# Stage two's operand moved to 98 partitions, written in 34- and 30-row transfers and read in one

## The chip, the cores and the metric

The kernel runs on one core of one Trainium2 chip. The metric is the device time of one execution in microseconds (us). A kernel is one program for five engines, each with an instruction order of its own: TensorE (PE, matmuls and weight loads), VectorE (DVE), ScalarE (ACT), GpSimd (POOL) and SyncE (SP). SP, ACT and GpSimd also issue the transfers, which 16 DMA engines carry out.

## The reference

The input x has 8 batches of 3072 x 256 numbers. Each batch goes through a Fourier transform along both axes, of which the real part is kept; every one of the 24,576 rows then goes through a layer of three parallel products.

```python
X = np.fft.fft(x, axis=1)
X = np.fft.fft(X, axis=2)
attn = X.real.astype(np.float32)            # (8, 3072, 256)
x = attn.reshape(24576, 256)
h = np.maximum(np.maximum(x @ w1, x @ w2), x @ w3)   # 256 -> 768
out = (h @ w_out).astype(np.float32)                 # 768 -> 256
```

## The kernel before

The transform along the 3072 rows is done in two stages, 96 x 32; the one along the 256 columns is folded into the weights (`product`, `prep_second`), as cosine and sine tables `md` and `nmd` times w1, w2 and w3. Only half of the spectrum is computed; the other half is a mirror image, for which the layer has a plus and a minus form (`unit_plus`, `unit_minus`).

A batch b passes these steps, which the class `Mix` holds:

- `load_x` (L106): GpSimd loads x into `xt`, in bf16, in two halves of two transfers (rows forward into partitions 0 to 31, reversed into 32 to 63). `mirror` (L113), on VectorE, fills partitions 64 to 127.
- `s` (L317), stage one: seven groups of matmuls with the small table `tabz`; ScalarE copies the sums to `tb`, 128 partitions: 64 rows q for even s, 64 for odd s, where s runs from 0 to 48.
- `y` (L329): SP writes `tb` to a DRAM buffer `db` of 49 x (64 x 128), in two transfers of 64 rows for each stretch of s, in packets of 256 B. The last 30 of the 64 rows are the sine part, the first 34 the cosine part (the sine part's first and last pair are zero and not stored).
- `z` (L338): SP reads `db` back into `yb`, now with s in the partitions: 49 rows of the cosine part from partition 0, 49 of the sine part from partition 64, each in a transfer of 48 rows and one of a single row. The partitions between are zero from the start.
- `x0` (L352): two small matmuls of the column 0 of x, into `x0s`; `c` (L361) copies `x0s` into column 0 of `yb`, on GpSimd (ScalarE for the first part of batch 0).
- `k` (L364) and `end`: stage two, matmuls of `yb` with the tables `te_tab` and `to_tab`, into `tE` and `tO`. The tables come from `angles` on VectorE and `tables` on ScalarE, in three parts of 512 columns.

The layer works on three blocks of 512 columns of tE and tO in each batch, six units each, so 18 units a batch. In a unit TensorE does the plus and minus matmuls (L388, L389, L396), ScalarE and VectorE take the maximum (L402, L403), and matmuls with `wout_bf` (L412) of the block before follow, ten at a time (`l2_some`). When a slot of 128 columns is done, VectorE adds it up into `ot` (L440, six buffers), GpSimd issues an indirect store of one half (L445) and sets a mark (L449), and SP issues the direct stores of the other (L452).

The order of all this is written out by hand, and each engine keeps it: `plan` gives to each unit what else is issued there. For batches 1 to 6 the steps for the next batch stand as follows (unit in front):

```python
ahead = {1: ("s0", "s1"), 2: ("s2", "y0", "s3"), 3: ("s4", "s5"), 4: ("s6", "y1", "x"),
         7: ("z",), 11: ("c",), **late}
```

`late` puts stage two into units 13 to 17; the x loads of the batch after next stand in units 9 to 12 and its mirrors in 14 to 17. In batch 0, preparing batch 1, they are later and closer: y0 in unit 7, y1 and x0 in 9, z in 11, c in 12.

The head of the program does the same for batch 0 in four stretches of s, with `warm_up` matmuls in TensorE's holes, makes the weight products of the first halves of w1, w2, w3 (`load_w(0)`), and loads the second halves (`load_w(1, landed[1])`) only when a read of `db` has landed. The products of the second halves (`prep_first`) and the tables of columns 512 on come in units 0 to 2 of batch 0.

Transfers of SP use eight completion semaphores in turn, so that a transfer waits for the one eight before it.

Of the kernel before, what the change touches and what calls it, by code (L numbers as in the profile page):

```python
# [10 lines left out]
BF16 = mybir.dt.bfloat16  # L11
INT32 = mybir.dt.int32
AX = mybir.ActivationFunctionType
ALU = mybir.AluOpType
# [29 lines left out]
def kernel(  # L44
# [9 lines left out]
    nc = tc.nc  # L54
# [6 lines left out]
    NHALF = 1536  # L61
    UNITS = 3 * NJC
    NS = 49
    RI = 17

    E_ = mybir.EngineType
    ctx.enter_context(tc.manual_schedule(
# [1 line left out]

    consts = ctx.enter_context(tc.tile_pool(name="consts", bufs=1))  # L70
    ps_f = ctx.enter_context(tc.tile_pool(name="ps_f", bufs=2, space=bass.MemoryType.PSUM))
    d_pool = ctx.enter_context(tc.tile_pool(name="dbuf", bufs=2, space=bass.MemoryType.DRAM))
    t_pool = ctx.enter_context(tc.tile_pool(name="tbuf", bufs=2))

    xt = [consts.tile([128, NS * 256], BF16, name=f"xt{i}", tag=f"xt{i}") for i in range(2)]
    xt = [t.rearrange("p (s d) -> p s d", d=256) for t in xt]
    tb = consts.tile([128, 25 * 128], BF16, tag="tb")
    tbv = tb.rearrange("p (s f) -> p s f", f=128)
    yb = consts.tile([128, 2 * RI * 128], BF16, tag="yb")
    x0s = consts.tile([128, RI], BF16, tag="x0s")  # L80
    ybv = yb.rearrange("p (r e f) -> p r e f", e=2, f=128)
    tabz = consts.tile([128, 192], BF16, tag="tabz")
    tab_at = [tabz[:, 64:192], tabz[:, 0:128]]
    tabx = consts.tile([128, 2 * RI], BF16, tag="tabx")
# [44 lines left out]
    pidx = gen.tile([128, 1], FP32, tag="pidx")  # L129
# [23 lines left out]
    kvec = gen.tile([128, NHALF + 1], FP32, tag="kvec")  # L153
# [12 lines left out]
         base=S + 1023, cm=-32)  # L166
    zero = gen.tile([128, 256], BF16, tag="zero")
    nc.vector.memset(zero, 0.0)
    for (p0, p1, step) in ((48, 64, 1), (112, 128, 1), (64, 112, 16)):
        cells = yb.rearrange("p (r c) -> p r c", c=256)[p0:p1, ::step, :]  # L170
        nc.sync.dma_start(out=cells, in_=zero[0:p1 - p0].unsqueeze(1).to_broadcast(
            [p1 - p0, (RI - 1) // step + 1, 256]))
    nc.vector.memset(x0s, 0.0)
    half_pi = gen.tile([128, 1], FP32, tag="half_pi")
    nc.vector.memset(half_pi, 0.5 * math.pi)
    nc.scalar.activation(out=half_pi, in_=half_pi, func=AX.Sin)
# [44 lines left out]
    for fc in range(2):  # L221
# [13 lines left out]
    _reduce(nc, vm, vm, qm, 256.0)  # L235
    nc.vector.tensor_copy(out=vm.rearrange("p (fc k c) -> p fc k c", fc=2, k=2)[:, :, :, 0],
                          in_=par.unsqueeze(1).to_broadcast([128, 2, 2]))
    phi = small("phi")
    scal(phi, up, 768.0, ALU.mult, 768.0, ALU.add)
    q = gen.tile([128, NHALF + 1], FP32, tag="q")  # L240
    step = float(2.0 * math.pi / 3072.0)

    def angles(c0, c1):
        cs = slice(c0, c1)
        scal(kvec[:, cs], kvec[:, cs], sidx, ALU.mult, phi, ALU.add)
# [63 lines left out]
    class Mix:  # L309

        def __init__(self, b):
            self.b = b
            self.x = xt[b % 2]
# [15 lines left out]
        def y(self, s0=0, s1=NS, engs=(nc.sync, nc.sync)):  # L329
            if s0 == 0:  # L330
                self.db = d_pool.tile([NS, 64 * 128], BF16, name="db", tag="db")
            dst = self.db.rearrange("s (q f) -> q s f", f=128)
            for hh in range(2):
                n = (s1 - s0 + 1 - hh) // 2
                engs[hh].dma_start(out=dst[:, s0 + hh:s1:2, :],
                                   in_=tbv[hh * 64:hh * 64 + 64, s0 // 2:s0 // 2 + n, :])

        def z(self, parts=(2,)):  # L338
            spans = {0: ((0, 6, 0), (1, 6, 17)), 1: ((6, 17, 6), (6, 16, 22)),
                     2: ((0, 17, 0), (1, 16, 17))}  # L340
            done = []
            for part in parts:
                for cs in range(2):
                    (i0, i1, c0) = spans[part][cs]
                    c1 = c0 + i1 - i0
                    for (a, z) in ((48, NS), (0, 48)):
                        done.append(nc.sync.dma_start(
                            out=yb[cs * 64 + a:cs * 64 + z, i0 * 256:i1 * 256],
                            in_=self.db[a:z, c0 * 256:c1 * 256]))
            return done  # L350

        def x0(self):  # L352
            psx = ps_f.tile([128, 512], FP32, name="psx", tag="ps")
            for cs in range(2):
                nc.tensor.matmul(psx[cs * 64:cs * 64 + NS, 0:RI], self.x[:, :, 0],
                                 tabx[:, cs * RI:(cs + 1) * RI], start=True, stop=True)
            for cs in range(2):
                nc.scalar.copy(out=x0s[cs * 64:cs * 64 + NS, :],
                               in_=psx[cs * 64:cs * 64 + NS, 0:RI])

        def c(self, i0=0, i1=RI, fn=nc.gpsimd.tensor_copy):  # L361
            fn(out=ybv[:, i0:i1, 1, 0], in_=x0s[:, i0:i1])

        def k(self, which, g):  # L364

            special = {0: [(0, 0, 32)], 1: [(0, 0, 16), (16, 16, 16)], 2: [(16, 0, 32)]}[g]
            parts = [(5 * g + 1 + i, 32 + 96 * i, 96) for i in range(5)] + special
            tab = (te_tab, to_tab)[which]
            ps2 = ps_f.tile([128, 512], FP32, name="ps2", tag="ps")
            for (r, c0, wd) in parts:  # L370
                nc.tensor.matmul(ps2[:, c0:c0 + wd], ybv[:, r, which, :],  # L371
                                 tab[:, g * 512 + c0:g * 512 + c0 + wd], start=True, stop=True)
            nc.scalar.copy(out=(self.tE, self.tO)[which][:, g * 512:(g + 1) * 512], in_=ps2)  # L373

        def end(self):
            ps3 = ps_f.tile([128, 512], FP32, name="ps3", tag="ps")
            for which, tab in enumerate((te_tab, to_tab)):
                nc.tensor.matmul(ps3[:, which:which + 1], ybv[:, 0, which, :],
                                 tab[:, NHALF:NHALF + 1], start=True, stop=True)
            nc.scalar.copy(out=t_mid[:, :, self.b], in_=ps3[:, 0:2])  # L380

    def unit_plus(te, to, jc, n):
# [152 lines left out]
    mirror(0, *FIRST[2])  # L535
    mirror(0, *FIRST[3])
    angles(0, 512)
    scal(sgn, pidx, 0.0, ALU.is_equal)
    scal(sgn, sgn, 2.0, ALU.mult, -1.0, ALU.add)
    scal(dif, sgn, 1.0, ALU.subtract)  # L540

    m = Mix(0)
# [8 lines left out]
    nc.scalar.activation(out=md_all, in_=vm, func=AX.Sin, scale=float(2.0 * math.pi / 256.0))  # L551
    nc.scalar.activation(out=nmd_all, in_=vm, func=AX.Sin, scale=float(-2.0 * math.pi / 256.0))
    m.s(4, pool=ps_s)
    m.y(32, 40)
    warm_up(2)
    m.s(5, pool=ps_s)
    m.s(6, pool=ps_s)
    m.y(40, NS)
    m.x0()
    tables(0, 512)  # L560
    landed = m.z((0, 1))
    warm_up(4)
    for half in range(2):
        keep_product(product(0, half, 0, ps_f, "ps"), 0, half, 0, dve)
    angles(512, 1024)
    for half in range(2):
        keep_product(product(1, half, 0, ps_s, "ps"), 1, half, 0, dve)
    warm_up(8)
# [16 lines left out]
                            in1=adj.unsqueeze(1).to_broadcast([128, B, 12]), op=ALU.add)  # L585
    dve(out=rows_m, in_=rows_f)

    load_w(1, landed[1])
    nc.gpsimd.dma_start(out=wout_bf.rearrange("p (jc c) -> p jc c", jc=NJC),
                              in_=moe_w_out.rearrange("(jc p) c -> p jc c", jc=NJC))  # L590
    HALVES = ((0, 25), (25, NS))
# [51 lines left out]
    def turn(b, ch):  # L643
        mirror(b, *CHUNKS[ch])

    for (u, fn) in ((0, lambda: next(second)), (0, lambda: tables(512, 1024)),
                    (1, lambda: next(first)), (1, lambda: next(first)),
                    (2, lambda: next(first)), (2, lambda: next(first)),
                    (2, lambda: m.c(6, RI)), (2, lambda: tables(1024, NHALF + 1)),
                    (3, lambda: m.k(0, 1)), (3, lambda: next(second)),  # L650
                    (4, lambda: m.k(1, 1)), (4, lambda: next(second)),
                    (5, lambda: next(second)),
                    (7, lambda: m.k(0, 2)), (8, lambda: m.k(1, 2)), (8, m.end)):
        at(0, u, fn)

# [93 lines left out]
```

## Time and profile before

| | |
|---|---|
| Median of 3 runs (lowest to highest) | 427.83 us (426.78 to 428.24) |
| Profiled execution | 428.37 us |
| Its span | 426.6 us (1.77 us lie around it) |
| Busy: PE, DVE, ACT, POOL | 399.3, 293.3, 254.7, 154.0 us |
| Transfers | 53.09 MB in 67582 packets, SP's queue 25.71 MB in 42980 |

Times in a timeline row are the start from the span's beginning and the length, in us; then come engine, line, operation, output and inputs, and how often; in brackets the idle time ahead of it on its engine and what ended it. SPq is SP issuing a transfer. A queue's row gives its packets, MB and the time its packets took as a share of 16 engines in that window; a row of transfers gives how many, and KB of each.

### The profile page before, as it was taken

How to read it: one execution, taken by the hardware profiler on the slowest of the kernel's cores; microseconds unless marked ns; L12 is line 12 of the kernel's file. 1: busy time of each engine (PE TensorE's matmuls, PEld its weight loads, DVE VectorE, ACT ScalarE, POOL GpSimd, SP SyncE). 2: the span in 40 equal slices, each digit the busy share in tenths (PEclk: the TensorE clock that was granted, in tenths of full speed). 3: DMA queues.
4: the chain of work that ended last, by engine and by line, in shares of the span. 5: the costliest groups of instructions: out<-in, count | busy, mean ns of one | idle time of the engine just before them, and what ended most of it. 6: DMA issues, size and time to landing. Idle time of an engine off the chain costs nothing.

```text
span 426.6 us, 8223 instructions
## 1 busy us (share of the span) xinstructions
PE 399.3 (94%) x2764; PEld 248.5 (58%) x2764; DVE 293.3 (69%) x528; ACT 254.7 (60%) x483; POOL 154.0 (36%) x258
## 2 busy tenths in 40 slices
PE   0977987999989999999999999999999999999996
PEld 0434554656656566556666666656666566666665
DVE  5876764767667667856767567847777576666773
ACT  1656564775566665766566665766566656655650
POOL 7381223423613145222723146313723243214420
PEclk9999999999999999999999999999999999999999
DMA  9999056954982369434992369434992464212324
GB/s 133 177 175 141 24 120 141 170 120 113 179 164 87 98 146 202 110 88 113 168 185 85 102 148 208 108 90 111 178 179 86 102 140 112 76 49 64 89 73 124
DMA packets 67582, 53.09 MB, mean 124 GB/s; under 512 B 35355, under 2 KB 63139, under 8 KB 66686
## 3 DMA queue, kind: packets, MB, share of 16 engines
q0 software_dynamic: 23856, 26.28, 30.4%
q1 hardware_dynamic: 42980, 25.71, 28.0%
q10 hardware_dynamic: 704, 0.59, 0.5%
q8 instruction: 21, 0.34, 0.3%
q14 instruction: 21, 0.16, 0.2%
HBM read 34.73 MB, written 31.59 MB: 155 GB/s over the span
## 4 chain that ended last, share of the span: by engine, by line
PE 74%; DMA 15%; DVE 4%; ACT 2%; issue 2%; POOL 1%; SPq 1%; DVEq 0%; POOLq 0%; ACTq 0%
PE po L412 25%; PE pse L388 12%; PE pse L396 12%; PE pse L389 12%; DMA xt<-in_x_dram 7%; PE ps L321 5%; PE po L435 4%; DMA out_dram<-ot 4%; DMA yb<-db 2%; PE pl L427 2%; DMA w_bf<-in_moe_w_dram 2%; PE ps L371 2%; DMA db<-tb 1%; DVE hm L403 1%; DVE ot L440 1%
## 5 line engine op out<-in xcount | busy, mean ns | idle before, releaser
L402 ACT ACTIVATE stmp<-pse 128x512 bf16<-128x512 f32 x288 | 169.6, 601 | 82.0 <-PE pse L389 71.5
L445 POOL DMA_INDIRECT out_dram<-ot,rows_m x92 | 105.4, 1145 | 242.0 <-DVE ot L440 226.8
L403 DVE TENSOR_TENSOR hp<-pse,stmp 128x512 bf16<-128x512 f32 x144 | 99.5, 691 | 106.8 <-PE pse L396 55.3
L388 PE MATMUL pse<-tE,gE 128*128 128x512 bf16 x288 | 109.1, 379 | 4.7 <-DVE hm L403 2.9
L389 PE MATMUL pse<-tO,gO 128*128 128x512 bf16 x288 | 109.1, 379 | 0.1
L403 DVE TENSOR_TENSOR hm<-pse,stmp 128x512 bf16<-128x512 f32 x144 | 98.9, 687 | 1.0 <-ACT stmp L402 0.9
L412 PE MATMUL po<-wout_bf,hp 128*128 128x256 bf16 x576 | 86.1, 273 | 0.0
L396 PE MATMUL pse<-tO,gD 128*128 128x512 bf16 x288 | 85.6, 379 | 0.0
L412 PE MATMUL po<-wout_bf,hm 128*128 128x256 bf16 x576 | 78.6, 273 | 0.0
L412 PEld LDWEIGHTS <-hp 128*128 128x128 bf16 x576 | 56.3, 98 | 26.1
L412 PEld LDWEIGHTS <-hm 128*128 128x128 bf16 x576 | 56.4, 98 | 16.3
L440 DVE TENSOR_TENSOR ot<-po,even 128x512 f32<-128x512 f32 x92 | 62.8, 682 | 0.2
L396 PEld LDWEIGHTS <-gD 128*128 128x128 bf16 x288 | 27.6, 98 | 32.0
L389 PEld LDWEIGHTS <-gO 128*128 128x128 bf16 x288 | 28.0, 97 | 27.5 <-issue 6.8
L323 ACT CAST tb<-ps 128x512 bf16<-128x512 f32 x48 | 26.3, 588 | 28.4 <-PE ps L321 28.4
L388 PEld LDWEIGHTS <-gE 128*128 128x128 bf16 x288 | 28.0, 97 | 22.3 <-issue 0.8
L321 PE MATMUL ps<-xt,tabz 128*128 128x512 bf16 x96 | 26.6, 397 | 12.0 <-DVE xt L117 11.4
L435 PE MATMUL po<-gw,tO 128*128 128x512 bf16 x92 | 34.9, 379 | 0.0
L116 DVE COPY xt<-xt 64x1524 bf16<-64x1524 bf16 (+4 forms) x32 | 19.3, 605 | 13.3 <-DMA xt<-in_x_dram 12.6
L431 ACT COPY even<-pl 128x512 f32<-128x512 f32 x46 | 27.0, 587 | 0.0
L373 ACT CAST tE<-ps 128x512 bf16<-128x512 f32 x24 | 14.1, 587 | 17.3 <-PE ps L371 17.3
L373 ACT CAST tO<-ps 128x512 bf16<-128x512 f32 x24 | 14.0, 585 | 16.6 <-PE ps L371 9.1
(130 smaller groups left out, 228.0 us busy)
## 6 DMA issues: line engine op xcount, KB each, us to landing
out_dram<-ot SPq DMA_DIRECT2D x71, 96.0 KB
xt<-in_x_dram POOLq DMA_DIRECT2D x14, 384.0 KB, 10.4
db<-tb SPq DMA_DIRECT2D x21, 192.0 KB
out_dram<-ot SPq DMA_DIRECT2D x48, 64.0 KB
yb<-db SPq DMA_DIRECT2D x7, 408.0 KB
xt<-in_x_dram POOLq DMA_DIRECT2D x7, 400.0 KB, 8.1
xt<-in_x_dram POOLq DMA_DIRECT2D x7, 368.0 KB
yb<-db SPq DMA_DIRECT2D x7, 360.0 KB
```

The source lines that it names most:

```text
L321: nc.tensor.matmul(ps1, tab_at[hh], self.x[:, 8 * k + hh:8 * k + 8:2, 0:128], start=(hh == 0), stop=(hh == 1))
L373: nc.scalar.copy(out=(self.tE, self.tO)[which][:, g * 512:(g + 1) * 512], in_=ps2)
L388: nc.tensor.matmul(pse[:, 0:n], gE[i][:, js], te, start=True, stop=False)
L389: nc.tensor.matmul(pse[:, 0:n], gO[i][:, js], to, start=False, stop=True)
L396: nc.tensor.matmul(pse, gD[i][:, js], to, start=False, stop=True, skip_group_check=True)
L402: nc.scalar.activation(out=stmp[:, 0:n], in_=pses[0][:, 0:n], func=AX.Relu)
L403: nc.vector.tensor_tensor(out=dst, in0=src3, in1=stmp[:, 0:n], op=ALU.max)
L412: nc.tensor.matmul(po, hcols(jc), wout_bf[:, jc * 256:(jc + 1) * 256], start=False, stop=(jc == NJC - 1), skip_group_check=True)
L431: nc.scalar.copy(out=even, in_=pl)
L435: nc.tensor.matmul(po, to[:, cp], gw[:, 256:768], start=True, stop=True)
L440: nc.vector.tensor_tensor(out=ot.rearrange("p (h c) -> p h c", h=2), in0=po.rearrange("p (h c) -> p h c", h=2), in1=lin.unsqueeze(1).to_br ...
L445: stored(nc.gpsimd.indirect_dma_start(out, bass.IndirectOffsetOnAxis(ap=rows_m[0:128 - lo, b * 12 + slot: b * 12 + slot + 1], axis=0), ot[ ...
```

## The change

Stage two's operand `yb` has 98 partitions in use instead of 128 with gaps: partition 2s + c holds row s of the cosine (c = 0) or sine part (c = 1). The tables get the same order: the angle's row number and phase come from the parity of the partition (`s_of`, `phi`), and the matmuls run over partitions 0 to 97. The DRAM buffers are two fixed ones of 49 x (4 x 17 x 128); two stretches of 256 numbers in each of their 49 rows, the sine part's first and last pair, are filled with zeros once, and the 64 rows of `tb` are written as 34 and 30, leaving room for the zeros: four transfers in `y` instead of two. `z` is one transfer of 98 rows instead of four.

For `x0`, the column 0 of x must reach even and odd partitions: GpSimd copies it (128x49) to every second column of `x0u`, zero elsewhere, and two matmuls with 98 columns, shifted by one, add up in one PSUM area; one ScalarE copy follows instead of two.

In the head, the loads of the weights' second halves wait for the last transfer of the third write (s from 32 to 40) instead of for a read, and stand ahead of the gD copies in GpSimd's order. The second third of the tables is made in the head instead of unit 0; several steps of units 0 to 5 of batch 0 move up by about one unit.

```diff
-    for (p0, p1, step) in ((48, 64, 1), (112, 128, 1), (64, 112, 16)):
...
+    for db in dbs:
+        pads = db[:, 2 * RI * 128:].rearrange("s (r c) -> s r c", c=256)[:, 0::16, :]
+        nc.sync.dma_start(out=pads, in_=zero[0:NS].unsqueeze(1).to_broadcast([NS, 2, 256]))
+    nc.vector.memset(x0u, 0.0)
...
+    scal(phi, par[:, 1:2], 12.0, ALU.mult, 768.0, ALU.add)
+    scal(s_of, par[:, 1:2], -1.0 / 64.0, ALU.mult)
+    nc.vector.tensor_tensor(out=s_of, in0=s_of, in1=pidx, op=ALU.add)
+    scal(s_of, s_of, 0.5, ALU.mult)
...
             for hh in range(2):
                 n = (s1 - s0 + 1 - hh) // 2
-                engs[hh].dma_start(out=dst[:, s0 + hh:s1:2, :],
-                                   in_=tbv[hh * 64:hh * 64 + 64, s0 // 2:s0 // 2 + n, :])
+                for (q0, q1, c0) in ((0, 2 * RI, 0), (2 * RI, 64, 2 * RI + 2)):
+                    done.append(nc.sync.dma_start(
+                        out=dst[c0:c0 + q1 - q0, s0 + hh:s1:2, :],
+                        in_=tbv[hh * 64 + q0:hh * 64 + q1, s0 // 2:s0 // 2 + n, :]))
...
+        def z(self, i0=0, i1=RI, eng=nc.sync):
+            rows = self.db.rearrange("s (c q) -> (s c) q", c=2)
+            return eng.dma_start(out=yb[0:KS, i0 * 256:i1 * 256], in_=rows[:, i0 * 256:i1 * 256])
 
         def x0(self):
+            nc.gpsimd.tensor_copy(x0u[:, 1:KS + 1:2], self.x[0:128, :, 0])
             psx = ps_f.tile([128, 512], FP32, name="psx", tag="ps")
             for cs in range(2):
-                nc.tensor.matmul(psx[cs * 64:cs * 64 + NS, 0:RI], self.x[:, :, 0],
-                                 tabx[:, cs * RI:(cs + 1) * RI], start=True, stop=True)
-            for cs in range(2):
-                nc.scalar.copy(out=x0s[cs * 64:cs * 64 + NS, :],
-                               in_=psx[cs * 64:cs * 64 + NS, 0:RI])
+                nc.tensor.matmul(psx[0:KS, 0:RI], x0u[:, 1 - cs:KS + 1 - cs],
+                                 tabx[:, cs * RI:(cs + 1) * RI], start=(cs == 0), stop=(cs == 1))
+            nc.scalar.copy(out=x0s[0:KS, :], in_=psx[0:KS, 0:RI])
...
+    angles(512, 1024)
...
-    m.y(32, 40)
+    early = m.y(32, 40)
...
-    landed = m.z((0, 1))
+    m.z(0, 6)
+    m.z(6, RI)
+    load_w(1, early[-1])
...
-    angles(512, 1024)
+    tables(512, 1024)
...
-    load_w(1, landed[1])
...
-    for (u, fn) in ((0, lambda: next(second)), (0, lambda: tables(512, 1024)),
+    for (u, fn) in ((0, lambda: next(second)), (0, lambda: next(first)),
                     (1, lambda: next(first)), (1, lambda: next(first)),
-                    (2, lambda: next(first)), (2, lambda: next(first)),
-                    (2, lambda: m.c(6, RI)), (2, lambda: tables(1024, NHALF + 1)),
-                    (3, lambda: m.k(0, 1)), (3, lambda: next(second)),
-                    (4, lambda: m.k(1, 1)), (4, lambda: next(second)),
-                    (5, lambda: next(second)),
+                    (2, lambda: next(first)), (2, lambda: m.c(6, RI)),
+                    (2, lambda: m.k(0, 1)), (2, lambda: tables(1024, NHALF + 1)),
+                    (3, lambda: m.k(1, 1)), (3, lambda: next(second)),
+                    (4, lambda: next(second)), (5, lambda: next(second)),
```

More of the change, by code (lines that the diff above doesn't have):

```diff
@@ L64 @@
     RI = 17
+    KS = 2 * NS
     E_ = mybir.EngineType
@@ L71 @@
     ps_f = ctx.enter_context(tc.tile_pool(name="ps_f", bufs=2, space=bass.MemoryType.PSUM))
-    d_pool = ctx.enter_context(tc.tile_pool(name="dbuf", bufs=2, space=bass.MemoryType.DRAM))
+    d_pool = ctx.enter_context(tc.tile_pool(name="dbuf", bufs=1, space=bass.MemoryType.DRAM))
+    dbs = [d_pool.tile([NS, 4 * RI * 128], BF16, name=f"db{i}", tag=f"db{i}") for i in range(2)]
     t_pool = ctx.enter_context(tc.tile_pool(name="tbuf", bufs=2))
@@ L80 @@
     x0s = consts.tile([128, RI], BF16, tag="x0s")
+    x0u = consts.tile([128, KS + 1], BF16, tag="x0u")
     ybv = yb.rearrange("p (r e f) -> p r e f", e=2, f=128)
@@ L168 @@
     nc.vector.memset(zero, 0.0)
-    for (p0, p1, step) in ((48, 64, 1), (112, 128, 1), (64, 112, 16)):
[L170 to L173, printed above, removed]
+    for db in dbs:
+        pads = db[:, 2 * RI * 128:].rearrange("s (r c) -> s r c", c=256)[:, 0::16, :]
+        nc.sync.dma_start(out=pads, in_=zero[0:NS].unsqueeze(1).to_broadcast([NS, 2, 256]))
+    nc.vector.memset(x0u, 0.0)
     half_pi = gen.tile([128, 1], FP32, tag="half_pi")
@@ L237 @@
                           in_=par.unsqueeze(1).to_broadcast([128, 2, 2]))
-    phi = small("phi")
-    scal(phi, up, 768.0, ALU.mult, 768.0, ALU.add)
+    phi, s_of = small("phi"), small("s_of")
+    scal(phi, par[:, 1:2], 12.0, ALU.mult, 768.0, ALU.add)
+    scal(s_of, par[:, 1:2], -1.0 / 64.0, ALU.mult)
+    nc.vector.tensor_tensor(out=s_of, in0=s_of, in1=pidx, op=ALU.add)
+    scal(s_of, s_of, 0.5, ALU.mult)
     q = gen.tile([128, NHALF + 1], FP32, tag="q")
@@ L244, in angles @@
         cs = slice(c0, c1)
-        scal(kvec[:, cs], kvec[:, cs], sidx, ALU.mult, phi, ALU.add)
+        scal(kvec[:, cs], kvec[:, cs], s_of, ALU.mult, phi, ALU.add)
         _reduce(nc, kvec[:, cs], kvec[:, cs], q[:, cs], 3072.0)
@@ L312, in __init__ @@
             self.b = b
-            self.x = xt[b % 2]
+            self.x, self.db = xt[b % 2], dbs[b % 2]
             self.tE = t_pool.tile([128, NHALF], BF16, name="tE", tag="tE")
@@ L327, in s, with y @@
                 evict(out=tbv[0:64, 24, :], in_=ps1[0:64, 0:128])
-        def y(self, s0=0, s1=NS, engs=(nc.sync, nc.sync)):
-            if s0 == 0:
-                self.db = d_pool.tile([NS, 64 * 128], BF16, name="db", tag="db")
+        def y(self, s0=0, s1=NS):
             dst = self.db.rearrange("s (q f) -> q s f", f=128)
+            done = []
             for hh in range(2):
                 n = (s1 - s0 + 1 - hh) // 2
-                engs[hh].dma_start(out=dst[:, s0 + hh:s1:2, :],
-                                   in_=tbv[hh * 64:hh * 64 + 64, s0 // 2:s0 // 2 + n, :])
@@ L338, in z @@
[L338 to L342, printed above, removed]
-                for cs in range(2):
[L344 to L349, printed above, removed]
-            return done
+                for (q0, q1, c0) in ((0, 2 * RI, 0), (2 * RI, 64, 2 * RI + 2)):
+                    done.append(nc.sync.dma_start(
+                        out=dst[c0:c0 + q1 - q0, s0 + hh:s1:2, :],
+                        in_=tbv[hh * 64 + q0:hh * 64 + q1, s0 // 2:s0 // 2 + n, :]))
@@ L357, in x0 @@
-            for cs in range(2):
-                nc.scalar.copy(out=x0s[cs * 64:cs * 64 + NS, :],
-                               in_=psx[cs * 64:cs * 64 + NS, 0:RI])
+                nc.tensor.matmul(psx[0:KS, 0:RI], x0u[:, 1 - cs:KS + 1 - cs],
+                                 tabx[:, cs * RI:(cs + 1) * RI], start=(cs == 0), stop=(cs == 1))
+            nc.scalar.copy(out=x0s[0:KS, :], in_=psx[0:KS, 0:RI])
         def c(self, i0=0, i1=RI, fn=nc.gpsimd.tensor_copy):
-            fn(out=ybv[:, i0:i1, 1, 0], in_=x0s[:, i0:i1])
+            fn(out=ybv[0:KS, i0:i1, 1, 0], in_=x0s[0:KS, i0:i1])
@@ L370, in k @@
             for (r, c0, wd) in parts:
-                nc.tensor.matmul(ps2[:, c0:c0 + wd], ybv[:, r, which, :],
-                                 tab[:, g * 512 + c0:g * 512 + c0 + wd], start=True, stop=True)
+                nc.tensor.matmul(ps2[:, c0:c0 + wd], ybv[0:KS, r, which, :],
+                                 tab[0:KS, g * 512 + c0:g * 512 + c0 + wd], start=True, stop=True)
             nc.scalar.copy(out=(self.tE, self.tO)[which][:, g * 512:(g + 1) * 512], in_=ps2)
@@ L377, in end @@
             for which, tab in enumerate((te_tab, to_tab)):
-                nc.tensor.matmul(ps3[:, which:which + 1], ybv[:, 0, which, :],
-                                 tab[:, NHALF:NHALF + 1], start=True, stop=True)
+                nc.tensor.matmul(ps3[:, which:which + 1], ybv[0:KS, 0, which, :],
+                                 tab[0:KS, NHALF:NHALF + 1], start=True, stop=True)
             nc.scalar.copy(out=t_mid[:, :, self.b], in_=ps3[:, 0:2])
```

## The prediction

> **What bounds the kernel.** I read the busy tenths first, then the queues and issues, then the timeline of the head and of two later batches.
>
> ```profile
> PE   0977987999989999999999999999999999999996
> ```
>
> TensorE is nearly full from the eighth slice on, so a wait put into its order there is lost time; only the head has holes.
>
> ```profile
> 12.41 7.30 SPq L335 DMA_DIRECT2D db<-tb  x8
> 20.68 2.94 SPq L347 DMA_DIRECT2D yb<-db  x8
> 24.66 0.39 PE L371 MATMUL ps<-te_tab,yb 128*128 128x96 bf16 x6 [1.76 <-DMA yb<-db]
> ```
>
> The head runs tb, write, db, read, yb, and TensorE waits for it until 24.66. The same trip one batch later, and in a settled batch:
>
> ```profile
> 51.52 1.28 SPq L335 DMA_DIRECT2D db<-tb  x2
> 58.91 1.32 SPq L335 DMA_DIRECT2D db<-tb  x2
> 63.14 1.51 SPq L347 DMA_DIRECT2D yb<-db  x4
> 71.01 0.40 PE L371 MATMUL ps<-te_tab,yb 128*128 128x96 bf16 x6 [2.72 <-DMA yb<-db]
> ...
> 140.36 1.32 SPq L335 DMA_DIRECT2D db<-tb  x2
> 147.76 1.35 SPq L335 DMA_DIRECT2D db<-tb  x2
> 154.93 1.30 SPq L347 DMA_DIRECT2D yb<-db  x4
> ```
>
> Batch 1 has no slack (2.72 us waited). The settled batch has some: its read has landed by about 161, the copy behind it runs at 163.74 on GpSimd, stage two starts at 167.45. Now the queue:
>
> ```profile
> q1 hardware_dynamic: 42980, 25.71, 28.0%
> ...
> out_dram<-ot SPq DMA_DIRECT2D x1, 8.0 KB
> ...
> yb<-db SPq DMA_DIRECT2D x7, 8.5 KB
> yb<-db SPq DMA_DIRECT2D x7, 7.5 KB
> ```
>
> and alone in 141:144, the two writes of half a batch, 64 rows each:
>
> ```profile
> q1 hardware_dynamic: 1568, 0.39, 62.4%
> ```
>
> They are 2 x 64 x 12 = 1536 packets of 256 B; 32 are left, one completion for each of 16 engines and each transfer. Duration: 0.624 x 16 x 3 us / 1536 = 19.5 ns. Over the whole run the shapes give 38,842 data packets (25,088 of db writes, 12,232 stored rows, 882 read rows, 640 of zeros), so 4,138 completions. SP issues 276 transfers; at 16 each that is 4,416, 278 too many. The 18 reads of one row and the one store of 8 rows explain it exactly if they use 1 and 8 engines: 18 x 15 + 8 = 278. All others have 16, 32, 48, 64 or 96 rows. So in every transfer here the engines got equal numbers of rows.
>
> **Part 1: writes of 34 and 30 rows.** Each write of 64 rows becomes one of 34 and one of 30. Equal shares of 34 rows among at most 16 engines means 2 engines (17 rows each); 30 rows use 15, the 98-row read 14, 7 rows each. No transfer of the trace has such a count, so the other reading (16 engines, uneven shares) stays a rival. I take equal shares because 276 of 276 fit them.
>
> [...]
>
> Two engines then carry 34 x 49 / 2 = 833 packets of a batch, plus 30 x 49 / 15 = 98: 931 x 19.5 ns = 18.2 us, against 196 packets and 3.8 us now. No row shows two engines working alone; should part of the 19.5 ns come from sixteen at once, it falls, and x loads beside it raise it: I allow 17 to 22 ns.
>
> Head: db packets start near 16 us; the last lands at 16 + 18.2 = 34.2, where now it is about 21. SP has 16 issues of some 0.6 us instead of 8, and later ones wait for earlier transfers' semaphores; both hide behind the two busy engines. The weights' second halves wait for the third write's last transfer, (304 + 304 + 152) x 19.5 ns = 14.8 us after 16, so near 31 instead of 24.2, and then share the two engines with the fourth write: 0 to 3 us, I take 1.5. So 35.7. Behind that wait on GpSimd stand the gD copies, wout and batch 1's x loads, 7 to 9 us later than now; stage two, which needs them, is later by more. From last packet to first stage-two matmul it is now 24.66 - 21 = 3.7 us with eight issues; with two issues I take 3.0. Stage two starts at 38.7, 14.0 later. Given back: the two waits for w (1.4 us, at 29.09 and 32.93), and about 1.1 of the 1.3 us that L388 waits for ACT behind the tables, since the middle table now runs while TensorE waits: 2.5. Added: TensorE idles 15 us, and its first eleven matmuls after the idle start (9.90 to 14.7) came 0.42 us apart instead of 0.216, 2.3 us. Head: 14.0 - 2.5 + 2.3 = 13.8, bounds 9 and 17.
>
> Batch 1: half a batch is 408 to 425 packets of 34-row writes on each of the two engines and 48 to 50 of the others: 8.9 and 9.3 us. First packets 1.3 us after the issue (now too), so the first half ends near 61.9 on today's clock, the second, issued at 58.91, waits for it and for a store and lands near 71.7. SP stands at the read's wait until then, with the stores behind it; six ot buffers cover that, as a slot comes every 4 us. Reading 98 rows on 14 engines: today's 98 rows take 5.8 us, I take 5 (7 rows of 0.33 to 0.74 us: 2.3 to 5.2), plus 0.9. Copy and matmul then come near 78.8 instead of 71.01: 7.8, bounds 4 and 11.
>
> Settled batches: first half ends 10.4 us after 140.36, the second at about 20.8, the read lands at 26 to 27.5; stage two begins at 27.1 plus the wait of part 2 (2.6), so TensorE doesn't wait for it. GpSimd's copy can stand up to 1.4 us, and the read now meets x loads that came after it. x is already late there (VectorE waits 1.8 to 2.9 us for it at L116 in the rows of batches 1 to 3), so I add 0.7 a batch, bounds 0 and 1.7: six batches, 4, bounds 0 and 10.
>
> **Part 2: x0 on GpSimd.** x0() now starts with a GpSimd copy of 128x49 into x0u, and the matmul of TensorE waits for it. Where that copy stands is told by the orders: behind the seventh indirect store of the batch, in GpSimd's order.
>
> ```profile
> 241.90 0.28 PE L355 MATMUL psx<-tabx,xt 128*49 128x17 bf16 x2
> 241.95 0.68 DVE L440 TENSOR_TENSOR ot<-po,even 128x512 f32<-128x512 f32 x1
> 242.90 0.97 POOL L445 DMA_INDIRECT out_dram<-ot,rows_m  x1 [2.19 <-DVE ot L440]
> 243.87 0.09 POOL L449 MEMSET mark<- 1x1 f32 x1
> ```
>
> TensorE runs psx at 241.90 and goes on with L388. After the change it stands there until the store is issued (243.87), the mark set (243.96) and x0u copied. The copies of 128x11 and 128x17 to yb took 0.23 and 0.26 to 0.31 us; by that slope 49 columns take 0.74, by the gD row (384 columns, 1.24) 0.33; I take 0.5. TensorE resumes at 244.5: 2.6 us lost, and nothing else can fill its order. The same rows stand at 96.75, 145.76, 193.96, 289.32 and 337.16: six batches, 15.6 us, bounds 0 (were the store's issue out of the way) and 17.4. In batch 1's preparation (58.39) it costs 1.5, which lies inside the 7.8.
>
> **Part 3: the rest, at nothing.** The read is one issue instead of four (1.3 us of SP, off the path). Matmuls on 98 rows have the same columns. Zero pads: two transfers before 12 us instead of three. Three more tiny VectorE steps (0.15 each) and the angles moved ahead lie beside the writes; without that cover, 0.45 and 2.1 us. k(0, 1) and k(1, 1) a unit earlier keep their matmuls.
>
> **Sum** on the profiled execution (428.37: span 426.6 and 1.77 around it): 13.8 + 7.8 + 4 + 15.6 = 41 gives 469.6; the median, 427.83, is 0.54 lower: 469.
>
> **Rivals.** A: one term is off, x0u is not waited for: 469 - 16 = 453, plus what the read then makes TensorE wait, 0 to 3. For it: only that another placing of copy and store would free it; against: the two orders. B: 34 rows go over 16 engines. Writes stay near 4 us a batch, the head loses some 2 us to eight more SP issues and wins them back from earlier weights; x0u stays: 428 + 15.6 + 1.5 = 445. For it: no row of 34 was seen. C, the other side: B's spread, and GpSimd's copy done before TensorE comes to psx. Then the weights issued at about 20 instead of 24.2 end the 1.4 us of w waits, the early table 1.1, and the single read about 1 us of batch 1's 2.72: 424. It decides if the copy runs ahead of the store that ends at 243.96. D: the two engines are the bound in every batch. Their load is 18.2 us and of the rest (0.62 busy of a 48 us batch, less 3.8 of writes) 26, together 44 of 48; if x loads slow the packets to 25 ns it is 49 and more waits appear: 480 to 488. For it the small margin, against it that writes and x loads lie in different parts of a batch.
>
> **Numbers.** Forecast 0.64, A 0.08, B 0.14, C 0.04, D 0.10. Forecast's own bounds: 428 + (9 + 4 + 0 + 14) = 455 to 428 + (17 + 11 + 10 + 17) = 483. The range takes B and most of D: 443 to 487. A measurement here tells 0.3% (1.3 us) from no change. Faster is C with a trifle, 0.05; same 0.01; slower 0.94.
>
> **What would show it.** Right: db packets until past 33 us in the head; completions of SP's queue far fewer than 16 a transfer; stage two first at 36 to 41; psx with an idle of 2 to 3 us released by GpSimd in batches 1 to 6; batch 1's stage two waiting some 10 us for yb. Wrong: a write of 34 rows done in about 2 us, or psx following the matmul before it without a gap.

## The result and the profile after

| | before | after |
|---|---|---|
| Median, lowest to highest of 4 runs, us | 427.37 (426.78 to 428.24) | 468.52 (466.0 to 469.99) |
| Profiled execution and its span, us | 428.37, 426.6 | 466.0, 464.1 |
| Mean granted clock of TensorE | 1.00 | 0.961 |

The changed kernel takes 1.0955 times as long (95% interval 1.0902 to 1.1008), 41 us more by the medians. The profiled execution is the shortest of the four, so the two traces differ by less: 37.5 us of span.

The busy tenths of TensorE, and the granted clock under them, from the page of after:

```profile
PE   2709878399899989998999989998998989999996
...
PEclk9958999599999999999899989998999999999999
```

A slice is 11.6 us. TensorE has a hole in the third slice (the head), one in the eighth (batch 1), and from there on an 8 about every four slices, one a batch, where before had nines. The clock falls to 5 in or behind the two deep holes and to 8 beside some of the shallow ones.

The head in the timeline of after (the four writes, the weights' loads, the read, first matmul of stage two), with batch 1 and a settled batch behind it:

```profile
10.94 15.68 SPq L340 DMA_DIRECT2D db<-tb  x16
26.62 2.14 POOL L148 DMA_DIRECT2D w_bf<-in_moe_w_dram  x3 [10.55 <-DMA db<-tb]
28.81 0.76 SPq L347 DMA_DIRECT2D yb<-db  x2
34.51 0.61 PE L367 MATMUL ps<-te_tab,yb 98*128 98x96 bf16 x6 [12.42 <-DMA yb<-db]
...
61.57 11.88 SPq L340 DMA_DIRECT2D db<-tb  x4
74.51 6.64 SPq L340 DMA_DIRECT2D db<-tb  x4
83.51 0.32 SPq L347 DMA_DIRECT2D yb<-db  x1
88.72 0.61 PE L367 MATMUL ps<-te_tab,yb 98*128 98x96 bf16 x6 [9.15 <-DMA yb<-db]
...
161.78 5.64 SPq L340 DMA_DIRECT2D db<-tb  x4
169.68 6.13 SPq L340 DMA_DIRECT2D db<-tb  x4
178.63 0.32 SPq L347 DMA_DIRECT2D yb<-db  x1
```

Stage two waits 12.42 us in the head and 9.15 in batch 1 (1.76 and 2.72 before). In the settled batch the four writes of a half keep SP for 5.6 to 6.1 us, where two kept it 1.32.

SP's queue on the page of after, and its activity alone in 14 to 28 us (the DMA row is the mean busy share of all 16 engines in 40 slices of that window):

```profile
q1 hardware_dynamic: 42358, 25.89, 21.7%
```

```profile
DMA  9997245211118111117211117313312411511421
...
q1 hardware_dynamic: 3223, 0.79, 25.7%
```

The count settles how many engines the writes used. The data are 38,398 packets (25,088 of db, 12,232 stored rows, 882 read rows, 196 of zeros). If each transfer adds one completion for each engine in use, then 36 writes of 34 rows on 2 engines, 36 of 30 on 15, 9 reads on 14, 2 fills of 49 rows on 7, 200 stores on 16 and one on 8 make 72 + 540 + 126 + 14 + 3,200 + 8 = 3,960, and 38,398 + 3,960 is 42,358, the page's number to the packet. The DMA row shows it too: behind the nines at its start (loads of GpSimd's queue) and between short peaks (the 30-row writes) it stands at 1, a tenth, where two engines of sixteen would give 0.125.

A settled batch around the x0 step, timeline of after:

```profile
268.20 0.68 DVE L436 TENSOR_TENSOR ot<-po,even 128x512 f32<-128x512 f32 x1
269.16 0.97 POOL L441 DMA_INDIRECT out_dram<-ot,rows_m  x1 [2.19 <-DVE ot L436]
270.13 0.09 POOL L445 MEMSET mark<- 1x1 f32 x1
270.16 0.27 POOL L350 COPY x0u<-xt 128x49 bf16<-128x49 bf16 x1
270.48 0.26 PE L353 MATMUL psx<-tabx,x0u 128*98 128x17 bf16 x2 [2.26 <-POOL x0u L350]
```

The psx matmul now stands 2.26 us, behind sum, store, mark and copy, in each of batches 2 to 7, and 1.89 in batch 1. What follows such a wait is seen in the busy times by stretches of 3.41 us, in batch 3 and in batch 4 (window, its length, then PE, PEld, DVE, ACT, POOL busy, PEclk, DMA share, GB/s):

```profile
165.25:168.66 3.41, 2.00 (x14) 1.17 (x12) 1.89 (x3) 1.53 (x4) 1.22 (x3) 1.00 0.42 108
168.66:172.07 3.41, 2.56 (x19) 1.74 (x20) 1.19 (x2) 1.37 (x3) 0.80 (x3) 1.00 0.45 124
...
216.45:219.86 3.41, 1.15 (x9) 0.60 (x8) 1.11 (x2) 0.44 (x2) 1.27 (x3) 1.00 0.53 145
219.86:223.27 3.41, 3.41 (x15) 1.86 (x13) 1.38 (x2) 1.20 (x2) 0.00 (x0) 0.50 0.35 87
```

In batch 3 the wait ended at 169.51 and the clock stayed at 1.00. In batch 4 TensorE was back at work at 219.16 and fully busy, but from 219.86 to 223.27 its clock was half. How the two waits differ stands in the last section.

**Where the 37.5 us lie.** The same matmuls in both traces give the lateness of after at each point. First matmul of stage two: 9.9 us late; end of batch 0's stage two: 10.1; psx of batch 1: 11.4; its stage two: 17.7; the end of that: 20.1; psx of batches 2 to 7: 22.4, 23.8, 25.2, 28.6, 32.5, 37.7; the end of the span: 37.5. From psx to psx, batches 2 to 7 lie 50.4, 49.7, 51.3, 51.3 and 53.1 us apart; before they lay 49.0, 48.2, 47.9, 47.4 and 47.8.

### The profile page after: what moved, and what is told of

Read it like the earlier page. It is cut to its first block, busy times and chain, and to the rows that moved or that the text cites. A ratio compares the mean times of both kernels' runs of the same rounds, so it can differ in the third digit from the quotient of the medians.

```text
span 464.1 us, 8199 instructions
## 1 busy us (share of the span) xinstructions
PE 406.9 (88%) x2764; PEld 251.3 (54%) x2764; DVE 293.7 (63%) x531; ACT 253.6 (55%) x475; POOL 155.7 (34%) x266
## 3 DMA queue, kind: packets, MB, share of 16 engines
q0 software_dynamic: 23856, 26.28, 28.4%
q1 hardware_dynamic: 42358, 25.89, 21.7%
## 4 chain that ended last, share of the span: by engine, by line
issue 32%; PE 31%; POOL 14%; DMA 11%; SPq 4%; DVE 3%; ACT 3%; POOLq 0%; DVEq 0%; ACTq 0%
POOL out_dram L441 11%; PE po L408 10%; DMA out_dram<-ot,rows_m 6%; PE pse L384 5%; PE pse L385 5%; PE pse L392 5%; SPq L340 4%; DMA yb<-db 2%; POOL xt L114 2%; DMA db<-tb 2%; DMA xt<-in_x_dram 1%; PE po L431 1%; ACT stmp L398 1%; POOL mark L445 1%; PE pl L423 1%
## 5 line engine op out<-in xcount | busy, mean ns | idle before, releaser
L384 PE MATMUL pse<-tE,gE 128*128 128x512 bf16 x288 | 110.5, 384 | 3.6 <-DVE hm L399 2.3
L385 PE MATMUL pse<-tO,gO 128*128 128x512 bf16 x288 | 110.9, 385 | 0.0
L408 PE MATMUL po<-wout_bf,hp 128*128 128x256 bf16 x576 | 87.9, 277 | 0.0
L392 PE MATMUL pse<-tO,gD 128*128 128x512 bf16 x288 | 87.6, 386 | 0.0
L408 PE MATMUL po<-wout_bf,hm 128*128 128x256 bf16 x576 | 80.5, 277 | 0.0
L408 PEld LDWEIGHTS <-hm 128*128 128x128 bf16 x576 | 57.5, 100 | 17.5
L328 ACT CAST tb<-ps 128x512 bf16<-128x512 f32 x48 | 26.2, 588 | 27.5 <-PE ps L326 27.5
L384 PEld LDWEIGHTS <-gE 128*128 128x128 bf16 x288 | 28.3, 98 | 22.4 <-issue 1.3
L326 PE MATMUL ps<-xt,tabz 128*128 128x512 bf16 x96 | 26.0, 389 | 12.1 <-DVE xt L120 11.5
L367 PEld LDWEIGHTS <-yb 98*128 98x128 bf16 x304 | 17.6, 99 | 24.3 <-DMA yb<-db 22.3
L367 PE MATMUL ps<-te_tab,yb 98*128 98x96 bf16 (+2 forms) x152 | 10.0, 204 | 21.6 <-DMA yb<-db 21.6
```

The lines of the kernel that those rows point to most:

```text
L328: evict(out=tb[:, k * 512:(k + 1) * 512], in_=ps1)
L367: nc.tensor.matmul(ps2[:, c0:c0 + wd], ybv[0:KS, r, which, :], tab[0:KS, g * 512 + c0:g * 512 + c0 + wd], start=True, stop=True)
L384: nc.tensor.matmul(pse[:, 0:n], gE[i][:, js], te, start=True, stop=False)
L385: nc.tensor.matmul(pse[:, 0:n], gO[i][:, js], to, start=False, stop=True)
L392: nc.tensor.matmul(pse, gD[i][:, js], to, start=False, stop=True, skip_group_check=True)
L408: nc.tensor.matmul(po, hcols(jc), wout_bf[:, jc * 256:(jc + 1) * 256], start=False, stop=(jc == NJC - 1), skip_group_check=True)
```

## Experiments

The disputed points were the number of engines and their pace, where x0u's wait sits and what it costs, what comes back when one of the two is gone, and what the early weights are worth. Each ratio is to the kernel before on the same chip. In short:

| run | 34-row writes | x0u late | median us | ratio (95%) |
|---|---|---|---|---|
| after | yes | yes | 468.52 | 1.0955 (1.0902 to 1.1008) |
| a_xe | yes | no | 462.87 | 1.0815 (1.0760 to 1.0870) |
| a_w3 | no | yes | 452.46 | 1.0524 (1.0473 to 1.0574) |
| a_w3_xe | no | no | 431.87 | 1.0039 (0.9999 to 1.0078) |

**1. Before, with the split alone (b_split34).** Only the row counts of the writes change, no address and no order:

```diff
-                engs[hh].dma_start(out=dst[:, s0 + hh:s1:2, :],
-                                   in_=tbv[hh * 64:hh * 64 + 64, s0 // 2:s0 // 2 + n, :])
+                for (q0, q1) in ((0, 34), (34, 64)):
+                    engs[hh].dma_start(out=dst[q0:q1, s0 + hh:s1:2, :],
+                                       in_=tbv[hh * 64 + q0:hh * 64 + q1, s0 // 2:s0 // 2 + n, :])
```

> The kernel before, with only its writes of db split into 34 and 30 rows (layout, reads, x0 and the order of the weights as before). Theory 1, engines get equal numbers of rows, so 34 rows keep to 2 engines: SP's queue has 43,016 packets (36 transfers of 64 rows become 36 of 34 and 36 of 30, 2 and 15 completions each: 4,138 - 576 + 612 = 4,174); two engines write a batch of the head in 13 to 15 us, stage two first at 33 instead of 24.7, batch 1 waits for yb some 9 us instead of 2.7, and the granted clock is halved for a while behind both waits: 427.4 + 8.7 + 2.3 + 10 = 448, 444 to 453. Rival, sixteen engines with uneven shares and only the additional issues of SP cost: 43,556 packets, 429 to 433.

Measured: 460.61 us, ratio 1.0724 (1.0697 to 1.0752). From the page, and from the waits of TensorE in 100 to 450 us (total, times, longest):

```profile
q1 hardware_dynamic: 43016, 25.71, 24.2%
```

```profile
PE pse L389 <- DVE hm L404: 10.9, 5, 2.6
```

The packets are what 2 and 15 engines give: before's 42,980 with 2 + 15 completions for each of 36 writes instead of 16, 36 more; stage two first runs at 33.80 and waits 11.92 us in batch 1. What I had not expected is the second row: in settled batches TensorE waits five times for VectorE, 1.7 to 2.6 us each, behind x loads that land late: in the same stretch VectorE waits 18.5 us for x, 9.4 in before. The split alone costs 31 to 33 us, more than my 20.

**2. The same split into 32 and 32 (b_split32), and 3. into 36 and 28 (b_split36).** As many transfers as in run 1, other row counts.

```diff
-                for (q0, q1) in ((0, 34), (34, 64)):
+                for (q0, q1) in ((0, 32), (32, 64)):     # run 2
+                for (q0, q1) in ((0, 36), (36, 64)):     # run 3
```

> The same with 32 and 32 rows: as many issues of SP as with 34 and 30, but both counts divide by 16. Theory 1 (the row count sets the engines): 43,556 packets, writes as quick as before, only the head's additional issues and two issues before batch 1's read remain: 431, 428 to 433. Rival (the number of issues on SP is what costs): the time of the 34 and 30 split, 444 to 453.

> The kernel before with its writes split into 36 and 28 rows, neither of them a multiple of 16. Theory 1 (the engines are the largest number up to 16 that divides the rows): 12 and 14 engines, 4,138 - 576 + 36 x 26 = 4,498 completions, 43,340 packets on SP's queue, and about the time of 32 and 32, 428 to 434. Rival (only multiples of 16 are spread, all others fall to 2 engines or 1): the time of 34 and 30 or more, 455 to 470.

Measured: 429.85 us, ratio 1.0037 (1.0005 to 1.0069), and 430.26 us, ratio 1.0007 (0.9967 to 1.0046). The queue on the page of run 2:

```profile
q1 hardware_dynamic: 43556, 25.72, 27.7%
```

That is run 1's count with 16 + 16 completions for each pair of writes in place of 2 + 15 (36 x 15 = 540 more); run 3 has 43,340, as 12 + 14 engines give (36 x 9 = 324 more). So twice as many transfers cost nothing that stands out of the measurement by more than 0.7%, and uneven halves on 12 and 14 engines do no harm either: the loss of run 1 is the two engines.

**4. After, with 34 written as 32 and 2 (a_w3).**

```diff
-                for (q0, q1, c0) in ((0, 2 * RI, 0), (2 * RI, 64, 2 * RI + 2)):
+                for (q0, q1, c0) in ((0, 32, 0), (32, 34, 32), (34, 64, 36)):
```

> The kernel after, with the 34 rows written as 32 and 2 (so 32, 2 and 30: 16, 2 and 15 engines; the 2 rows hold 12 packets for each of two engines). Theory 1: half a batch is written in 2 to 3 us in place of 7, batch 1's wait for yb falls from 9.15 to about 3 us with the halved clock behind it, the head is then held by 24 issues of SP instead, stage two first near 29; x0's waits stay: 468.5 - 5 - 10 = 453, 448 to 458. Rival (the issues or the new layout of db cost, not the engines): 468 or more.

Measured: 452.46 us, ratio 1.0524 (1.0473 to 1.0574). From its timeline:

```profile
76.79 0.40 PE L367 MATMUL ps<-te_tab,yb 98*128 98x96 bf16 x6 [0.61 <-DMA yb<-db]
```

Batch 1's wait for the read is gone (0.61), the waits for x0u are all there (13.6 us in batches 2 to 7), and stage two in the head starts at 30.26: still 5.6 later than before, with all writes but the 2-row ones spread over 15 or 16 engines. Whether the 24 issues hold it or the weights that run beside the read, as in run 8, wasn't taken apart.

**5. After, with x0u's copy one unit earlier (a_xe).** The copy becomes a step of its own, in unit 3 (unit 8 of batch 0) ahead of the unit whose store it stood behind; the matmuls stay.

```diff
-            nc.gpsimd.tensor_copy(x0u[:, 1:KS + 1:2], self.x[0:128, :, 0])
+        def x0_copy(self):
+            nc.gpsimd.tensor_copy(x0u[:, 1:KS + 1:2], self.x[0:128, :, 0])
...
-    ahead = {1: ("s0", "s1"), 2: ("s2", "y0", "s3"), 3: ("s4", "s5"), 4: ("s6", "y1", "x"),
+    ahead = {1: ("s0", "s1"), 2: ("s2", "y0", "s3"), 3: ("xc", "s4", "s5"), 4: ("s6", "y1", "x"),
```

> The kernel after, with GpSimd's copy into x0u issued one unit earlier, ahead of the indirect store that stands before it now; the writes stay at 34 and 30. Theory 1 (TensorE's wait for x0u comes from that place in GpSimd's order): the six waits of 2.26 us in settled batches and batch 1's of 1.9 are gone, and so is the half clock behind three of them (about 2 us each): 468.5 - 14 - 6 = 449, 445 to 455. Rival (the reads of yb are late in settled batches too, and only hidden behind x0's wait): TensorE then waits for yb there, 455 to 465.

Measured: 462.87 us, ratio 1.0815 (1.0760 to 1.0870). From the waits of TensorE in 100 to 450 us, and one of VectorE's rows in the timeline:

```profile
PE pse L386 <- DVE hm L401: 9.1, 5, 2.3
PE ps L369 <- DMA yb<-db: 3.0, 2, 1.7
```

```profile
247.26 0.62 DVE L119 COPY xt<-xt 64x1651 bf16<-64x1651 bf16 x1 [3.55 <-DMA xt<-in_x_dram]
```

No wait for x0u is left, and 12.1 us of others stand in its place: five for VectorE, whose mirror of x waits for its load (3.55 us in this row, 17.1 over the stretch, against 9.2 in after), as in run 1, and two for the read. GpSimd's timeline shows what that load meets:

```profile
241.24 0.26 POOL L360 COPY yb<-x0s 98x17 bf16<-98x17 bf16 x1 [5.88 <-DMA yb<-db]
```

GpSimd's copy into `yb` waits for the read, here until 241.24 (22.1 us in five waits of the stretch, none in after). The writes are over by then: their last packet starts at 228.4. The read's packets run from 230.7 to 239.2, beside the x loads, of which the first is issued at 231.62. The load that the mirror waits for, issued at 234.02, has landed only at 247.26, 13.2 us later. In the same batch of after the read's last packet starts at 234.3, ahead of the first x load (235.00), and the mirror's load takes 9.0 us. So x meets the late read, not the writes, and the wait for x0u, which put the x loads some 2 us later, had kept the two apart. That the read slows the load is argued from the overlap.

**6. Both undone in after (a_w3_xe)**, runs 4 and 5 together, of whose diffs the two core lines are:

```diff
+                for (q0, q1, c0) in ((0, 32, 0), (32, 34, 32), (34, 64, 36)):
...
+    ahead = {1: ("s0", "s1"), 2: ("s2", "y0", "s3"), 3: ("xc", "s4", "s5"), 4: ("s6", "y1", "x"),
```

> The kernel after with both undone: 34 rows written as 32 and 2, and GpSimd's copy into x0u a unit earlier. Theory 1 (the two engines, x0's wait and the halved clock behind long waits are the whole loss): no wait of TensorE over 1.5 us after batch 0; what stays is the head, held by SP's 24 issues (stage two at about 30 instead of 24.7): 427.4 + 5.6 + 1 = 434, 431 to 438. Rival (98 partitions, the read on 14 engines or the table order cost something of their own): 440 to 450.

Measured: 431.87 us, ratio 1.0039 (0.9999 to 1.0078). Settled batches lie 47.2 us apart (the last pair 48.9), and VectorE's waits for x are back to 7.4 us. So the two causes hold all of the loss, up to 0.8%: the 98 partitions, the single read, the head's order and the other edits together cost at most about 3 us. That is a sum of both signs: stage two first runs at 29.05, 4.4 us later than before, and the settled batches win some 3 us back.

**7. After, with TensorE kept busy during the wait (a_fill).** Eight matmuls into psx, overwritten by the real ones, stand ahead of x0's matmuls in batches 1 to 7; they work on x and change no result.

```diff
+            if self.b:
+                for _ in range(8):
+                    nc.tensor.matmul(psx, tab_at[0], self.x[:, 0:8:2, 0:128], start=True, stop=True)
```

> The kernel after with eight more matmuls (their sums are overwritten by psx) ahead of x0's two, for batches 1 to 7: they fill 1.7 of the 2.26 us in which TensorE waits for x0u and leave the wait's end where it is. Theory 1 (behind a wait of 2.26 us the granted clock is halved in some batches, which costs about 2 us each time): the settled batches keep full clock, 468.5 - 6 to - 8 = 461, 458 to 465, mean clock up by 0.01 to 0.02. Rival (the clock falls there for another reason, or costs nothing as other engines set the pace): 467 to 470.

Measured: 460.39 us, ratio 1.0705 (1.0646 to 1.0764), 8 us less than after (11 by the ratios) although x0u comes no earlier. The granted clock on its page:

```profile
PEclk9966999779999999999999999999999999999999
```

Idle gaps are 0.54 us now, the clock never falls from batch 2 on, and batches lie 49.65 us apart, all of them: 47.2 and 2.45 for the step. Batch 1 still waits 9.33 for its read. So the low clock is a price of its own, beside the wait.

**8. Before, with the head's new order alone (b_order):** the weights' second halves behind the third write, ahead of the gD copies, the middle tables in the head, units 0 to 5 moved up.

```diff
-    m.y(32, 40)
+    early = m.y(32, 40)
...
-    landed = m.z((0, 1))
+    m.z((0, 1))
+    load_w(1, early)
...
-    angles(512, 1024)
+    tables(512, 1024)
...
-    load_w(1, landed[1])
...
-    for (u, fn) in ((0, lambda: next(second)), (0, lambda: tables(512, 1024)),
+    for (u, fn) in ((0, lambda: next(second)), (0, lambda: next(first)),
```

> The kernel before with only the head's new order: the loads of the weights' second halves behind the third write and ahead of the gD copies, the middle third of angles and tables in the head, the steps of units 0 to 5 as in the kernel after. Theory 1 (these take away the two waits for w, 1.4 us, and one of ACT behind the tables, 1.3 us): 427.4 - 2 = 425, 424 to 426.5. Rival (the weights' loads now run beside the last write and the read of yb and hold stage two up by as much): 427 to 430.

Measured: 430.98 us, ratio 1.0029 (1.0002 to 1.0056). From its timeline:

```profile
20.33 2.17 POOL L145 DMA_DIRECT2D w_bf<-in_moe_w_dram  x3 [6.45 <-DMA db<-tb]
...
26.62 0.39 PE L372 MATMUL ps<-te_tab,yb 128*128 128x96 bf16 x6 [3.83 <-DMA yb<-db]
```

The time that theory 1 forecast did not come. The weights are asked for at 20.33 instead of 24.2 and the two waits for them are gone, but stage two starts 2.0 us later (26.62 against 24.66) and batch 1's at 72.95 against 71.01. The weights' transfers now run beside the read that TensorE waits for. That they slow it is argued from the overlap; no run changed the load's size. The gain itself is there: behind the longer wait (3.83 us against 1.76) the clock is half from 27.7 to 31.1, which puts the layer's matmuls 4.0 us behind those of before, and by 37 us they are 1.8 behind. So some 2 us were given back, and the half clock had taken as much.

**9. A version after the findings (best).** The 98 partitions, zero pads and, but for the head's two, single reads stay. The 17 pairs stand in the order 6 to 15, 1 to 5, 0, 16, so that the sine part's two pads come last and 64 rows go in one transfer; x0u's copy is a unit earlier as in run 5; head, weights, tables and units 0 to 5 are as before.

```diff
+    AT = {**{r: r - 6 for r in range(6, 16)}, **{r: r + 9 for r in range(1, 6)}, 0: 15, 16: 16}
...
-                for (q0, q1, c0) in ((0, 2 * RI, 0), (2 * RI, 64, 2 * RI + 2)):
-                    done.append(nc.sync.dma_start(
-                        out=dst[c0:c0 + q1 - q0, s0 + hh:s1:2, :],
-                        in_=tbv[hh * 64 + q0:hh * 64 + q1, s0 // 2:s0 // 2 + n, :]))
+                done.append(nc.sync.dma_start(
+                    out=dst[0:64, s0 + hh:s1:2, :],
+                    in_=tbv[hh * 64:hh * 64 + 64, s0 // 2:s0 // 2 + n, :]))
```

> 98 partitions without either loss: the pairs of rows stand in another order (6 to 15, 1 to 5, 0, 16), so that the sine part's two zero pairs come last and the 64 rows of tb are written in one transfer again (two transfers in y, as before); one read of 98 rows (two in the head), GpSimd's copy into x0u a unit early; weights, tables and units in the order of the kernel before. Theory 1 (the new operand costs nothing by itself and its single read lands a little earlier, so that VectorE's waits for x in settled batches shrink; with both undone the settled batches took 47.2 us against 47.4 to 49.0): stage two first at about 24.5, 427.4 - 3 = 424, 422 to 426.5. Rival (the settled gain of that run came from its later head, which left x earlier in relation): 426.5 to 430.

Measured: 422.18 us (421.44 to 423.24), ratio 0.9889 (0.9862 to 0.9916): 1.1% less than before, with an interval clear of 1. Its queue has after's packets with 16 completions for each of 36 writes instead of 2 + 15 (36 fewer). From its page and its timeline:

```profile
q1 hardware_dynamic: 42322, 25.89, 24.2%
```

```profile
25.29 0.40 PE L371 MATMUL ps<-te_tab,yb 98*128 98x96 bf16 x6 [2.42 <-DMA yb<-db]
...
69.56 0.40 PE L371 MATMUL ps<-te_tab,yb 98*128 98x96 bf16 x6 [1.11 <-DMA yb<-db]
```

The head is 0.6 later than before, batch 1's wait 1.6 shorter, and settled batches lie 47.2 us apart (the last pair 48.6) instead of 47.4 to 49.0. Which of the kept edits brings the settled part wasn't taken apart.

## Why the prediction was right, and where it was wrong

The median came out at 468.5 where 469 was forecast, for the causes named. That the sum met it so closely is luck: its terms were off by -3.7, +2.2, -1.0 and -6 us, and half clock behind the settled waits, which it left out, gave 5.3.

| term of the sum | predicted | measured in the trace |
|---|---|---|
| head, to the end of batch 0's stage two | 13.8 | 10.1 |
| batch 1, to the end of its stage two | 7.8 | 10.0 |
| x0u's wait, batches 2 to 7 | 15.6 | 2.3 + 5 x 2.45 = 14.6 |
| late x loads, with other small waits | 4 | about -2 |
| half clock behind settled waits | not in the sum | 5.3 |
| sum | 41.2 | 38, against 37.5 of span |

The last rows come from the distances of the settled batches: over 49.65 (run 7) they have 0.7, 0, 1.7, 1.7 and 3.4 us. The low clock of three of them takes 1.7, 1.7 and 1.9; two waits for VectorE, 0.56 and 1.51, are the rest. Before, over 47.2, the same five had lost 4.4, hence the -2.

**Two engines: right.** The step from the completions of 8 rows and 1 row to 34 holds to the packet, in after and in runs 1, 3, 4 and 9 too (with 32 + 2 rows the count is 42,934, 576 more than after, 36 x 16). Rival B is out, and with it C.

**The pace: mis-sized.** "19.5 ns" a packet, taken from sixteen busy engines, was used as the time between two packets of one engine. In the head the 3,136 data packets, 931 on each of the two engines, start between 14.5 and 28.4 us: 15 ns each. The duration of a packet is still 0.257 x 16 x 14 / 3,136 = 18.4 ns, so packets overlap on an engine, and the pace lies outside my 17 to 22. The weights are asked for at 26.62 instead of "near 31", the read at 28.81. About 1.5 us of that come from an earlier start (14.5, not "near 16"), for which no cause is shown. In the settled batch from 161.78 the read's last packet starts 21.2 us behind the first issue, where I had 26 to 27.5.

**From the last packet to stage two: mis-sized the other way.** It took 28.4 to 34.51, 6.2 us, where I took 3.0: the read, issued at 28.81, runs beside the weights, wout and x loads that were queued at the same time. That these slow it is argued, as in run 8. The other two terms of the head were about right: the half clock (0.50 until 38.95) puts the layer's matmuls from 10.1 to 12.0 us behind those of before, 2.0 where I added 2.3, and by the end of batch 0's stage two they are back at 10.1, 1.9 given back where I had 2.5. So the head is 3.7 off because stage two starts 9.9 us later and not 14.0; had the pace and the way to stage two not erred in opposite directions, it would be further off.

**Batch 1: right in place, short of a term.** The wait for the read grows by 6.4 us (9.15 against 2.72) and x0u takes 1.4 to 1.9, together the predicted 7.8; about 2.3 more go by between the start and the end of that stage two, which runs at half clock (0.50 from 88.7 to 93.5). I had counted the half clock in the head only.

**x0u: right.** The place, behind the seventh store in GpSimd's order, is as told, and the cost is 2.26 of idle a batch against 2.6; the copy took 0.27 us and not 0.5.

**x loads: the step that failed.** I added 0.7 a batch to a batch that x0u had already made 2.3 longer. Runs 1 and 5 show that lateness of x is real with 34-row writes (10.9 and 9.1 us of waits of TensorE), and after, with 2.1 of them beside the wait for x0u, that this wait hides it: of the two, only the longer is paid. This is why the two causes don't add: by the ratios they cost 35 us (a_xe) and 22 (a_w3) one by one and 41 together. My expectations of runs 1 and 5 repeated the error, both too low by 12 to 14 us. The prediction had the place right, the read that now meets the x loads: in run 5 the read's packets lie beside them and the writes' do not. It missed that x0u's wait moves those loads out of the read's way.

**No wait for the read in settled batches: right** in after, where no such wait is listed beyond the head and batch 1, and only there: without x0u's 2.3 us run 5 has two. Rival D had this margin as small, and rightly so.

## What to carry to other kernels

Count the rows over which a transfer is shared out before splitting it: 34 rows ran on 2 engines, 32 on 16, and 31 to 33 us hung on that. The queue's packets less the data packets, 3,960 in after, told here how many engines were used. A small step on a helper engine is as late as what stands ahead of it in that engine's order: here a copy of 0.27 us cost TensorE, the busiest engine, 2.45 us a batch, and one unit earlier nothing. When two delays end at the same point, only the longer is paid, so price each as if the other were gone before adding them or hoping for one's removal.

## What the runs showed of the hardware

- **Half clock after short waits, by where they lie.** In the clock record of after, half clock begins six times: at 25.30 for 13.65 us, at 83.33 for 10.24, at 219.86, 271.06 and 322.26 for 3.41 each, and at 462.21 to the program's end. The later five begin 17, 57, 72, 87 and 128 times 3.413 us after the first. The waits of 2.26 us for x0u of batches 2 to 7 are six. Three, of batches 4 to 6, lay whole between two neighbouring points of this spacing (216.45 to 219.86 above), and half clock followed each. The other three were cut by such a point, into 0.58 and 1.68 us of idle, 1.41 and 0.85 (165.25 to 172.07 above), and 0.83 and 1.43, and none followed. The rest of this trace fits: of its 3.41 us stretches at full clock from 11.65 on, where the record begins, those with TensorE idle for 2.01 us or more (the length less the PE busy) were followed by half clock, those with 1.80 or less were not. No run moved a wait to test this. In run 4 the four waits for x0u of batches 2 to 5 were all followed by a slow stretch: matmuls of 512 columns came 0.42 to 0.43 us apart there instead of 0.21 to 0.22. In after the half clock cost 1.7 to 1.9 us each time, nearly as much as the wait; behind the 0.54 us of run 7 there was none.
- **SP took longer to issue a 30-row write behind a 34-row one.** In the half batches of after from 61 to 176 us, SP's issue of a 34-row write took 0.25 to 0.54 us, and the 30-row write behind it 2.0 to 3.1, where a write of 64 rows before took 0.58 to 0.70 from 51 to 149 us, and one 1.70. One of the 30-row writes in batch 1 took 8.8, which makes up most of that row's 11.88; why is open for all of them.
